# Moving two groups of activation tiles off the 64-byte grid of SBUF

## The chip, the cores and the metric

The kernel runs on one core of a Trainium2 chip. Its five engines are TensorE (PE in the profile; its weight loads are listed apart as PEld), VectorE (DVE), ScalarE (ACT), GpSimd (POOL) and SyncE (SP), and they work side by side, held in order by semaphores. The metric is the device time of one execution in microseconds; the median of several runs is given.

## The reference

Inputs are in float32, and the weights arrive as 64-bit values that the kernel decodes itself. Three stages follow one another over 8 batches of 576 rows with 512 features:

```python
# linear attention, 8 heads of 64
q_s = softmax(q, axis=-1); k_s = softmax(k, axis=2)
x = einsum('bhsd,bhde->bhse', q_s, einsum('bhsd,bhse->bhde', k_s, v))    # then heads side by side
# gated convolution
gate = sigmoid(causal_conv(x, conv_w))        # 5 taps along the sequence
y = (gate * (x @ w_val)) @ w_out
# channel mix; y_prev is y one row earlier
xk = mu_k * y + (1 - mu_k) * y_prev
xr = mu_r * y + (1 - mu_r) * y_prev
out = sigmoid(xr @ w_r) * (relu(xk @ w_k) ** 2 @ w_v)     # w_k: 512 x 1024, w_v: 1024 x 512
```

## The kernel before

The 4,608 rows are cut into 12 chunks of T = 384. Features lie on the 128 partitions, the rows of a chunk along the free axis, so a tile of activations is 128 x 384 and a chunk has 4 of them for 512 features.

The first chunk (i == 0) runs in float32 with one matmul for each product. For the other 11 chunks every operand a is split into a high part h (rounded to the type float32r, by ScalarE) and a low part l = a - h (by VectorE), and a product becomes three matmuls: h by h, h by l, l by h. `passes` (line 449) issues all of them, so almost every matmul of the kernel stands under line 449 and is told apart by its tiles. In the profile `ph<-xkh,wk_hi` is output, moving operand, stationary operand. Each matmul is preceded by a load of its own 128 x 128 stationary block.

The products of a chunk, in this order:

- **px** is the attention's output: moving operand q, stationary the attention's k-v matrix. It is copied to xf (5 taps need 4 earlier rows, so its data begins 4 words into the tile) and split into the pair xh, xl.
- **pv** is x by w_val: moving operand xh or xl, 384 columns. VectorE multiplies it with the gate into gf, which is split into gh, gl.
- **py** is the gated value by w_out: moving operand gh or gl, 384 columns. ScalarE copies it to yf (one earlier row ahead of the data). `mix` makes xm from it twice: for w_r, split into xrh, xrl, and for w_k, split into xkh, xkl.
- **racc** is xr by w_r: here the weights are the moving operand, 512 columns, and 128-column slices of xrh or xrl are stationary.
- **ph** is xk by w_k in 8 blocks: moving operand xkh or xkl, 384 columns. Relu and square give rf, split into kh, kl.
- **vacc** is the square by w_v: weights moving, 512 columns, slices of kh or kl stationary.

The main products of a chunk are issued in this order on TensorE; the attention of the next chunk, the convolution and the key-value rounds are put between them by two lists written by hand (`FRONT` for the start, `REST` for chunks 2 to 11).

Tiles are taken from pools by tag; each tag has a number of buffers of fixed place that are used in turn. Tag "x" (8 buffers in the pool `work`) holds xh, xl, and later in the same chunk xrh, xrl. Tag "g" (8 buffers, alone in the pool `gated`) holds gh, gl, and later xkh, xkl. In the first chunk single tiles of the same tags hold the whole values. Tags "q" and "k" are in `work` too. `pair_of` makes pairs, `one` single tiles. Pools on the left lie behind each other in SBUF in the order in which they are opened, and four tiles that nobody reads serve as gaps: left_gap, before_gap (ahead of the g tiles), behind_gap (behind them) and right_gap.

Of the kernel before, what the change touches and what calls it, by code (L numbers as in the profile page):

```python
# [8 lines left out]
F32 = mybir.dt.float32  # L9
F32R = mybir.dt.float32r  # L10
# [56 lines left out]
def tile_linear_attention_gated_conv_channel_mix(  # L67
# [21 lines left out]
    P = 128  # L89
    NC = DM // P  # L90
    NF = DFF // P
    T = 384
# [15 lines left out]
    work = ctx.enter_context(tc.tile_pool(name="work", bufs=1))  # L108
    gatep = ctx.enter_context(tc.tile_pool(name="gated", bufs=1))


    wts.tile([P, LEFT_GAP // 4], F32, name="left_gap")
    gatep.tile([P, 16], F32, name="before_gap")
    ends = ctx.enter_context(tc.tile_pool(name="ends", bufs=1, side="right"))
    ends.tile([P, RIGHT_GAP // 4], F32, name="right_gap")
    behind = ctx.enter_context(tc.tile_pool(name="behind", bufs=1))
    behind.tile([P, 48], F32, name="behind_gap")


    first_ctx = ctx.enter_context(ExitStack())  # L120
# [187 lines left out]
    def kv_max(st):  # L308
        kt = st["k"]
        pm = scratch("pm")[:, 0:HR * D]  # L310
        one = pm.rearrange("p (h d) -> p h d", d=D)
        nc.vector.tensor_max(one, kt[:, :, 0, :], kt[:, :, 1, :])
        for x in range(2, NST):
            nc.vector.tensor_max(one, one, kt[:, :, x, :])
        st["pm"] = pm
# [105 lines left out]
    def q_norm(st, h=slice(0, H)):  # L421
# [6 lines left out]
        nc.vector.reciprocal(qs, qs)  # L428
        nc.vector.tensor_mul(qt, qt, q4.rearrange("p t (h o) -> p t h o", o=1).to_broadcast([P, NT, n, D]))

    def pair_of(tag, bufs, pool=work):
        return lambda name: tuple(pool.tile([P, T], F32R, tag=tag, bufs=bufs, name=name + x) for x in "hl")

    x_pair, g_pair, q_pair, k_pair = pair_of("x", 8), pair_of("g", 8, gatep), pair_of("q", 2), pair_of("k", 8)

    def one(tag, bufs, name):
        return (gatep if tag == "g" else work).tile([P, T], F32, tag=tag, bufs=bufs, name=name)

    def split(a, pair):

# [40 lines left out]
    def x_take(st, i, c):  # L481
        pq = st["pq", c]
        if i < 2:
            qf, = st["q", c] = (one("q", 2, "q"),)
            if i:
                nc.scalar.copy(qf, pq[:, :T])
            else:
                nc.scalar.copy(
                    qf.rearrange("c (p t) -> c p t", t=NT), pq[:, :T].rearrange("c (t p) -> c p t", t=NT)
                )  # L490
            return
        qh, ql = st["q", c] = q_pair("q")
        nc.scalar.copy(qh, pq[:, :T])  # L493
        nc.vector.tensor_sub(ql, pq[:, :T], f32(qh))  # L494
# [313 lines left out]
```

## Time and profile before

| what | us |
|---|---|
| median of 3 runs | 812.14 |
| lowest and highest run | 810.77, 812.4 |
| span of the profiled execution, first to last instruction | 810.1 |
| TensorE busy in it | 798.3 |
| weight loads (overlap with TensorE's matmuls) | 701.2 |
| VectorE busy | 564.5 |
| ScalarE busy | 479.3 |
| GpSimd busy | 59.2 |

The profiled execution has no other time of its own than its span. Matmuls are pipelined: one starts before the recorded end of the one ahead of it, so the pace is read from start to start, or from a run of matmuls and its length, and not from the duration of one. Durations of one are given in ns, all else in us.

### The profile page before, as it was taken

What the parts mean: (1) busy time and instruction counts of PE and PEld (TensorE: products, weight loads), DVE (VectorE), ACT (ScalarE), POOL (GpSimd) and SP (SyncE); (2) the same over time, 40 slices, a digit from 0 to 9 for tenths busy, and PEclk for the clock granted to TensorE, in tenths of its full rate; (3) what the DMA queues carried; (4) which work ended last, traced back from release to release, by engine and by line L of the source; (5) the groups of instructions that cost most, each with busy time, mean ns of one, the idle gap of its engine ahead of it and who ended that gap; (6) DMA issues with size and microseconds to landing.
All of it is one profiled execution on the core that took longest, in us unless ns stands there. A gap on an engine that the chain in (4) does not pass through costs nothing.

```text
span 810.1 us, 12242 instructions
## 1 busy us (share of the span) xinstructions
PE 798.3 (99%) x4578; PEld 701.2 (87%) x4578; DVE 564.5 (70%) x1016; ACT 479.3 (59%) x948; POOL 59.2 (7%) x224
## 2 busy tenths in 40 slices
PE   6999999999999999999999999999999999999998
PEld 5545588999999999989989999999999999998996
DVE  7999889976777577577758577577576747644611
ACT  4667678637746746655754763763764674664542
POOL 2130001000002001000000100100000100100000
PEclk9999999999999999999999999999999999999999
DMA  9786220132222102013041211211222010000001
GB/s 310 244 269 217 59 78 1 40 98 59 75 63 59 40 27 72 7 36 91 7 98 46 53 40 39 60 39 40 59 65 73 1 37 23 22 1 14 26 1 40
DMA packets 92537, 53.25 MB, mean 66 GB/s; under 512 B 74018, under 2 KB 84286, under 8 KB 92478
## 3 DMA queue, kind: packets, MB, share of 16 engines
q1 hardware_dynamic: 92432, 52.44, 22.3%
q8 instruction: 36, 0.59, 0.3%
q14 instruction: 23, 0.19, 0.1%
q10 hardware_dynamic: 46, 0.02, 0.0%
HBM read 43.02 MB, written 9.44 MB: 65 GB/s over the span
## 4 chain that ended last, share of the span: by engine, by line
PE 95%; DMA 2%; DVE 1%; ACT 1%; SPq 1%; issue 0%; ACTq 0%
PE ph L449 25%; PE vacc L449 25%; PE racc L449 12%; PE pv L449 12%; PE py L449 12%; PE px L449 4%; PE kvacc L347 2%; PE pq L476 2%; DMA raw<-in_moe_w_val_dram 1%; DMA raw<-in_moe_w_k_dram 1%; DVE gate L548 1%; DMA kt<-in_k_dram 1%; PE mx L333 0%; PE pmT L321 0%; SPq L303 0%; DVE whole L152 0%
## 5 line engine op out<-in xcount | busy, mean ns | idle before, releaser
L548 DVE SCALAR_TENSOR_TENSOR gate<-xf,cw,gate 128x384 f32<-128x384 f32 x192 | 117.2, 615 | 5.1 <-ACT gate L546 2.3
L449 PE MATMUL ph<-xkh,wk_hi 128*128 128x384 f32 x352 | 120.3, 342 | 0.0
L449 PE MATMUL ph<-xkl,wk_hi 128*128 128x384 f32 x352 | 118.3, 336 | 0.0
L449 PE MATMUL ph<-xkh,lower 128*128 128x384 f32 x352 | 118.1, 336 | 0.0
L642 ACT ACTIVATE rf<-ph 128x384 f32<-128x384 f32 x96 | 46.8, 488 | 99.0 <-PE ph L449 98.1
L449 PE MATMUL vacc<-wv_hi,kh 128*128 128x512 f32 x264 | 104.0, 394 | 0.0
L449 PE MATMUL vacc<-lower,kh 128*128 128x512 f32 x264 | 103.2, 391 | 0.0
L449 PE MATMUL vacc<-wv_hi,kl 128*128 128x512 f32 x264 | 103.1, 391 | 0.0
L442 DVE TENSOR_TENSOR kl<-rf,kh 128x384 fp32r<-128x384 f32 x88 | 48.9, 556 | 70.1 <-ACT kh L441 69.1
L616 DVE SCALAR_TENSOR_TENSOR xm<-yf,mus,xm 128x384 f32<-128x384 f32 x96 | 56.5, 614 | 24.2 <-ACT xm L615 23.7
L449 PEld LDWEIGHTS ph<-xkh,wk_hi 128*128 128x128 f32 x352 | 66.2, 188 | 2.0 <-ACT xkh L441 0.2
L449 PEld LDWEIGHTS ph<-xkh,lower 128*128 128x128 f32 x352 | 66.2, 188 | 1.9
L449 PEld LDWEIGHTS ph<-xkl,wk_hi 128*128 128x128 f32 x352 | 66.1, 188 | 0.0
L494 DVE TENSOR_TENSOR ql<-pq,qh 128x384 fp32r<-128x384 f32 x40 | 22.2, 556 | 62.5 <-ACT qh L493 62.5
L441 ACT CAST gh<-gf 128x384 fp32r<-128x384 f32 x44 | 22.5, 511 | 72.0 <-DVE gf L589 72.0
L449 PE MATMUL py<-gh,wout_hi 128*128 128x384 f32 x176 | 59.6, 343 | 0.0
L449 PE MATMUL pv<-xh,lower 128*128 128x384 f32 x176 | 59.5, 338 | 0.0
L449 PE MATMUL pv<-xh,wval_hi 128*128 128x384 f32 x176 | 59.5, 338 | 0.0
L449 PE MATMUL pv<-xl,wval_hi 128*128 128x384 f32 x176 | 59.3, 337 | 0.0
L449 PEld LDWEIGHTS vacc<-wv_hi,kl 128*128 128x128 f32 x264 | 49.5, 188 | 11.0 <-DVE kl L442 0.3
L449 PE MATMUL py<-gl,wout_hi 128*128 128x384 f32 x176 | 58.2, 339 | 0.0
L449 PE MATMUL py<-gh,lower 128*128 128x384 f32 x176 | 58.0, 338 | 0.0
(132 smaller groups left out, 1723.0 us busy)
## 6 DMA issues: line engine op xcount, KB each, us to landing
out_dram<-rs SPq DMA_DIRECT2D x36, 256.0 KB, 2.0
kt<-in_k_dram SPq DMA_DIRECT2D x16, 512.0 KB, 4.5
qt<-in_q_dram SPq DMA_DIRECT2D x29, 256.0 KB, 3.4
vt<-in_v_dram SPq DMA_DIRECT2D x56, 128.0 KB, 3.6
raw<-in_moe_w_k_dram SPq DMA_DIRECT2D x8, 512.0 KB, 5.5
raw<-in_moe_w_v_dram SPq DMA_DIRECT2D x8, 512.0 KB, 6.8
raw<-in_moe_w_val_dram SPq DMA_DIRECT2D x4, 512.0 KB, 6.3
raw<-in_moe_w_out_dram SPq DMA_DIRECT2D x4, 512.0 KB, 8.4
```

The source lines that it names most:

```text
L347: nc.tensor.matmul(acc[e * D:(e + 1) * D, x * VW:(x + 1) * VW], lhsT=kt[:, 2 * x + e, s, :], rhs=st["v"][:, 2 * x + e, s, :], start=(s == ...
L441: nc.scalar.copy(pair[0], a)
L442: nc.vector.tensor_sub(pair[1], a, f32(pair[0]))
L449: nc.tensor.matmul(po, lhsT=left[a], rhs=right[b], start=start and x == 0, stop=stop and x == len(m) - 1)
L476: nc.tensor.transpose(pq[:, t * P:(t + 1) * P], qt[:, t, 2 * c:2 * c + 2, :].rearrange("p h d -> p (h d)"), f32(ident))
L494: nc.vector.tensor_sub(ql, pq[:, :T], f32(qh))
L548: nc.vector.scalar_tensor_tensor(out=gx(gate), in0=xv[:, :, HALO - sh:HALO - sh + L], scalar=tap(c, HALO - sh), in1=gx(gate), op0=ALU.mult ...
L616: nc.vector.scalar_tensor_tensor(out=gx(xf), in0=yv[:, :, 1:], scalar=mu[:, c:c + 1], in1=gx(xf), op0=ALU.mult, op1=ALU.add)
L642: nc.scalar.activation(rf, ph[:, :T], AF.Relu)
```

## The change

Tiles of tag "x" are made 16 words longer than their 384 words of data, and the data begins 4 words (16 bytes) into the tile. The gap ahead of the g tiles grows from 16 to 24 words and the gap behind them shrinks from 48 to 40, so the g tiles move by 32 bytes against what lies ahead of and behind their pool. The instructions, their order, the number of buffers and all waits stay as they are.

```diff
-    gatep.tile([P, 16], F32, name="before_gap")
+    gatep.tile([P, 24], F32, name="before_gap")
     ends = ctx.enter_context(tc.tile_pool(name="ends", bufs=1, side="right"))
     ends.tile([P, RIGHT_GAP // 4], F32, name="right_gap")
     behind = ctx.enter_context(tc.tile_pool(name="behind", bufs=1))
-    behind.tile([P, 48], F32, name="behind_gap")
+    behind.tile([P, 40], F32, name="behind_gap")
...
+    SHIFT = {"x": 4}
+
+    def shifted(pool, dtype, tag, bufs, name):
+
+        o = SHIFT.get(tag, 0)
+        return pool.tile([P, T + 4 * o], dtype, tag=tag, bufs=bufs, name=name)[:, o:o + T]
+
     def pair_of(tag, bufs, pool=work):
-        return lambda name: tuple(pool.tile([P, T], F32R, tag=tag, bufs=bufs, name=name + x) for x in "hl")
+        return lambda name: tuple(shifted(pool, F32R, tag, bufs, name + x) for x in "hl")
...
     def one(tag, bufs, name):
-        return (gatep if tag == "g" else work).tile([P, T], F32, tag=tag, bufs=bufs, name=name)
+        return shifted(gatep if tag == "g" else work, F32, tag, bufs, name)
```

## Rows read from the trace of the kernel before

**Rows 1.** Page, parts 1 and 4: busy time of TensorE; the chain's shares.

```profile
PE 798.3 (99%) x4578; PEld 701.2 (87%) x4578; DVE 564.5 (70%) x1016; ACT 479.3 (59%) x948; POOL 59.2 (7%) x224
...
PE 95%; DMA 2%; DVE 1%; ACT 1%; SPq 1%; issue 0%; ACTq 0%
PE ph L449 25%; PE vacc L449 25%; PE racc L449 12%; PE pv L449 12%; PE py L449 12%; PE px L449 4%; PE kvacc L347 2%; PE pq L476 2%; DMA raw<-in_moe_w_val_dram 1%; DMA raw<-in_moe_w_k_dram 1%; DVE gate L548 1%; DMA kt<-in_k_dram 1%; PE mx L333 0%; PE pmT L321 0%; SPq L303 0%; DVE whole L152 0%
```

**Rows 2.** Busy time by stretch; the first line names the columns.

```profile
core 0: us, PE busy (x) PEld busy (x) DVE busy (x) ACT busy (x) POOL busy (x), PEclk, DMA share, GB/s
...
160.00:800.00 640.00, 640.00 (x3797) 589.08 (x3796) 418.53 (x751) 369.75 (x740) 37.48 (x154) 1.00 0.16 43
```

**Rows 3.** Waits of weight loads: who for whom, us in total, times, longest.

```profile
PEld vacc L449 <- issue: 7.2, 30, 0.2
PEld racc L449 <- issue: 3.8, 16, 0.2
```

**Rows 4.** Chain that ended last, in order of time: start us, us, what.

```profile
60.11 6.13 PE ph L449 x19
...
686.50 8.32 PE pv L449 x48
694.82 8.47 PE py L449 x48
703.29 8.17 PE racc L449 x36
...
772.95 6.24 PE ph L449 x36
```

**Rows 5.** Timeline, 773.49 to 773.83 us: start us, us, engine, instruction.

```profile
773.49 0.33 PE L449 MATMUL ph<-xkh,lower 128*128 128x384 f32 x1
773.49 0.19 PEld L449 LDWEIGHTS ph<-xkl,wk_hi 128*128 128x128 f32 x1
773.65 0.34 PE L449 MATMUL ph<-xkl,wk_hi 128*128 128x384 f32 x1
773.66 0.19 PEld L449 LDWEIGHTS ph<-xkh,wk_hi 128*128 128x128 f32 x1
773.83 0.34 PE L449 MATMUL ph<-xkh,wk_hi 128*128 128x384 f32 x1
```

**Rows 6.** Views of tiles, elementwise work: ns min/median/max, first and last start us.

```profile
L514 ACT CAST xh<-xf x44: 501/515/536, 92.7 to 746.5; 128x384 fp32r<-128x384 f32 x44
L515 DVE TENSOR_TENSOR xl<-xf,xh x44: 550/552/569, 93.2 to 747.2; 128x384 fp32r<-128x384 f32 x44
...
L441 ACT CAST xkh<-xm x44: 496/510/518, 131.0 to 769.6; 128x384 fp32r<-128x384 f32 x44
L442 DVE TENSOR_TENSOR xkl<-xm,xkh x44: 547/556/559, 132.0 to 770.1; 128x384 fp32r<-128x384 f32 x44
...
L607 ACT ACTIVATE yf<-py x48: 469/492/495, 45.0 to 764.8; 128x384 f32<-128x384 f32 x48
...
L642 ACT ACTIVATE rf<-ph x96: 467/491/511, 64.3 to 799.9; 128x384 f32<-128x384 f32 x96
```

**Rows 7.** View of the tiles whole: float32 matmuls of the first chunk, columns as above.

```profile
L449 PE MATMUL ph<-xm,whole x64: 486/486/488, 58.4 to 97.6; 128*128 128x384 f32 x64
...
L449 PE MATMUL pv<-xf,whole x32: 486/486/590, 21.2 to 35.8; 128*128 128x384 f32 x32
...
L449 PE MATMUL py<-gf,whole x32: 486/486/590, 36.2 to 46.4; 128*128 128x384 f32 x32
```

**Rows 8.** Views of tiles: full-rate matmuls, one of three groups of each product.

```profile
L449 PE MATMUL pv<-xl,wval_hi x176: 334/334/422, 107.6 to 756.0; 128*128 128x384 f32 x176
...
L449 PE MATMUL py<-gh,wout_hi x176: 332/336/445, 115.6 to 764.1; 128*128 128x384 f32 x176
...
L449 PE MATMUL racc<-wr_hi,xrh x132: 389/389/397, 124.5 to 772.1; 128*128 128x512 f32 x132
...
L449 PE MATMUL ph<-xkh,wk_hi x352: 332/336/445, 133.1 to 799.2; 128*128 128x384 f32 x176
```

## The prediction

> **What bounds the kernel now.** I read the page first. TensorE is busy for 798.3 of 810.1 us, and the chain that ended last is PE for 95% of the span, almost all of it line 449, the helper that issues the products [rows 1]. The table of stretches then shows that this is no average over different limits: from 160 to 800 us PE is busy for all of 640.0 us, VectorE for 418.5, ScalarE for 369.8, and the clock granted to PE is 1.00 of full speed, its 2.4 GHz level [rows 2]. Of the waits of weight loads the longest in total, 7.2 us in 30 pieces, is one for nothing but the issue [rows 3]. So for this change the time is a count of matmuls times the pace of one, and what VectorE or ScalarE do faster or slower costs nothing until PE has to wait for it.
>
> The pace of one matmul is read from the chain in order of time, where a run of matmuls stands with its length. 36 of ph take 6.24 us, so 173.3 ns from one start to the next, 48 of pv take 8.32 us, also 173.3, and 36 of racc take 8.17 us, 226.9 [rows 4]. At 2.4 GHz 384 columns would pass in 160.0 ns and 512 in 213.3. Each matmul thus costs 13.3 to 13.6 ns, 32 clocks, more than its columns, and that excess is the same for both widths. The 20 single-pass products of the first chunk (float32, which runs at half the column rate, so 320.0 ns for 384 columns) do not show it: 19 take 6.13 us, 322.6 each, an excess of 2.6 ns [rows 4]. The timeline shows what goes on during the excess: each weight load starts within 0.01 us of the matmul before its own and takes 0.19 us, so one is always reading SBUF while PE streams the moving operand at full rate [rows 5]. My reading, an inference, is that the two streams of PE get in each other's way: 32 clocks for each load, and nearly nothing when the moving stream runs at half the rate.
>
> **The change part by part.** Adding up the tiles in the order of the code, every operand of a full-rate matmul now starts on a multiple of 64 bytes: x tiles at 132,608 + 1,536 n, g tiles at 157,248 + 1,536 n, weights on multiples of 256. Afterwards x starts 16 bytes past the grid (a tile is 64 bytes longer, so the step between tiles is 1,600 bytes), g 32 bytes past it (the gap ahead grows by 32, the one behind shrinks by 32). All that lies behind x moves by 512 bytes, so k, kvf and the upper weights stay on the grid. No instruction, transfer, wait or buffer is added or removed.
>
> Elementwise work on shifted tiles: nothing. The same subtraction takes a median of 552 ns (xl, whose source xf starts 16 or 48 bytes past the grid) and 556 ns (xkl, both sources on it) [rows 6]. ScalarE's cast takes 515 ns from the off-grid xf and 510 from xm, on the grid [rows 6]. As a destination: yf, written at 4 bytes past a multiple of 32, takes 492 ns from PSUM, rf, on the grid, 491 [rows 6]. Both signs stay within 5 ns; it hides under PE, of whose window these engines fill 65% and 58% [rows 2]. Without that cover 5 ns on the casts and subtractions that write x or g (eight groups of 44, four of them in [rows 6]) would be 1.8 us; I take 0.
>
> Products of the first chunk that read x or g in float32: nothing. pv there reads xf 16 or 48 bytes off the grid and takes a median of 486 ns, py and ph on the grid 486 as well [rows 7]. At half rate the start makes no difference.
>
> Full-rate products with x or g as moving operand are the change. pv is 3 x 176 = 528 matmuls on x; py is 528 and ph 3 x 352 = 1,056 on g, so 1,584 [rows 8]. No row has such a matmul off the grid, so its price is bounded. At best the excess falls to that of the half-rate rows: 13.3 - 2.6 = 10.7 ns on 2,112 matmuls, -22.6 us. At worst a row of 1,536 bytes that touches 25 groups of 64 bytes instead of 24 pays for the extra group: 16 columns, 6.7 ns, +14.1 us. Between the two I take the shift itself: the moving stream meets the load's reads 16 bytes, 4 columns, 1.67 ns elsewhere for x, and 8 columns, 3.33 ns for g. That size has a neighbour in the trace: one and the same ph matmul takes 332 ns at least and 336 in the median, though every operand is on the grid [rows 8], and one step in the timeline reads 0.16 us, where 173.3 ns must read 0.17 or 0.18 [rows 5]. So where in each other the two streams start is worth some 4 ns. For the sign I take a gain, which is an assumption: with both streams on the grid, each load runs the longest it can in step with the moving stream. Terms: 528 x 1.67 = 0.9 us, 1,584 x 3.33 = 5.3 us.
>
> racc: 396 matmuls with x as stationary operand and weights as moving [rows 8]. There the load moves and the stream stays: 1.67 ns either way, 0.7 us. I take 0.
>
> The sum is -6.2 us. Against the profiled execution's span of 810.1 us that gives 803.9; its time is not listed apart from the span, and the median of the three runs, 812.14, stands 2.0 us above it, so the forecast is 812.1 - 6.2 = 806.0 us. Nothing is late instead: in py, the products that wait for VectorE's gf and its split, 48 matmuls take 8.47 us, 0.15 us over pv's [rows 4], and that wait starts at pv's end whatever pv's pace is.
>
> [...]
>
> **The rivals.** *No change: the streams settle into one pace whatever the start.* For it: pv's x tiles lie on multiples of 128 bytes, ph's g tiles 64 past one, and both take 173.3 ns [rows 4]; the short step in the timeline is made up for in the next one, 0.18 us [rows 5]. Against it: all those starts are equal modulo 64, which is what changes now. Time: 812.1 us. [...]
>
> *Slower: the 25th group.* If PE fetches 64 bytes at a time, an off-grid row needs one fetch more for each matmul, 16 clocks: 2,112 x 6.67 ns = 14.1 us, 826.2 us; half hidden, 819. It decides from 0.77 ns per matmul (1.6 us over 2,112). For it: at full rate there is no slack, the stream is what sets the pace. Against it: the half-rate pv with an off-grid xf shows none of it, 486 against 486 ns [rows 7].
>
> *The edit does not shift what counts*, because the excess is not the meeting of two reads but a fixed price of changing weights at this data type; then the time is that of the first rival, 812.1. Against it: half-rate products change weights as often and pay 2.6 ns [rows 4].
>
> **How the numbers follow.** The gain has a chance of 0.49 (its own range is 797 to 810: a few tenths of a us up to two and a half times the sum), no change 0.29 with both reasons for it, the extra fetch 0.22. A measurement of this kernel can tell about 0.2%, 1.6 us, from no change, so these are also the chances of faster, same and slower. The likeliest is 806.0. The range runs from 797 to 819: it leaves out the part of the gain that nears the half-rate bound, some 0.07, and the extra fetch where none of it hides, some 0.11.
>
> **What would show it.** In the chain in order of time, ph and py would fall from 173.3 to about 170 ns per matmul and pv to 171.7, with racc at 226.9 and vacc unchanged. The medians of ph's and py's rows would fall by 3 to 4 ns, those of xkl, gl and the casts by nothing. ph at 180 would be the extra fetch; ph at 173.3 with steps still settling would be the first rival. The prediction is wrong if the streams' relative start decides nothing, or if x and g answer with opposite signs: then -0.9 and +5.3 or the reverse would have to be read apart. A new wait of weight loads for VectorE or ScalarE of more than a microsecond would say that elementwise work, which I cost at nothing, has come onto the path.

## The result: 1% slower, with the sign of the forecast turned

The changed kernel takes 820.12 us (median of 4 runs, 819.36 to 820.55) against 812.25 for the kernel before; the ratio is 1.0099, 95% interval 1.0085 to 1.0113. The forecast was 806.0 us, with a range of 797 to 819 and a chance of 0.22 for slower. The profiled execution has a time of 819.36 and a span of 817.4 us, 7.3 more than before. Of the experiments below one run, the profiled one of e10, took 1,621.34 us, about twice its other four; it is left out of e10's ratio, and e10's chain is read from a further run of the same kernel, e12.

The page of the changed kernel, parts 1 and 4, against [rows 1]:

```profile
PE 806.5 (99%) x4578; PEld 706.8 (86%) x4578; DVE 564.7 (69%) x1016; ACT 479.6 (59%) x948; POOL 58.2 (7%) x224
...
PE 98%; ACT 0%; DVE 0%; issue 0%
PE ph L456 25%; PE vacc L456 25%; PE py L456 13%; PE pv L456 13%; PE racc L456 13%; PE px L456 3%; PE kvacc L347 3%; PE pq L483 2%; PE heat L745 1%; PE pmT L321 0%; PE mx L333 0%; ACT q L495 0%; DVE rs L666 0%; DVE pm L314 0%; DVE raw L151 0%
```

The same 4,578 matmuls keep PE busy 8.2 us longer; VectorE and ScalarE work as long as before, to 0.3 us. Line 449 is line 456 now. Waits of weight loads are where they were, against [rows 3]:

```profile
PEld vacc L456 <- issue: 7.2, 30, 0.2
PEld racc L456 <- issue: 3.8, 16, 0.2
```

So it is the pace. The chain in order of time, last chunk (start us, us, what), against [rows 4]:

```profile
754.35 8.42 PE pv L456 x48
762.77 8.59 PE py L456 x48
771.36 8.38 PE racc L456 x36
779.74 6.36 PE ph L456 x36
786.09 2.08 PE vacc L456 x9
...
807.09 6.44 PE vacc L456 x27
```

ph went from 173.3 to 176.7 ns (6.36 us / 36), pv to 175.4, py by 2.5 ns, and racc, in which no moving operand was shifted, from 226.9 to 232.8 ns. vacc, whose operands are on the grid before and after, takes 2.08 us for the 9 matmuls behind the 36 of ph where before, in the same place of the chunk, the chain has

```profile
779.19 2.05 PE vacc L449 x9
...
799.86 6.44 PE vacc L449 x27
```

and 6.44 us for 27 in both: vacc loses a little at its beginning and nothing later. The groups by line and form (count | busy us, mean ns of one) give the amounts; here the three groups of ph, after and then before:

```profile
L456 PE MATMUL ph<-xkh,wk_hi 128*128 128x384 f32 x352 | 121.4, 345 | 0.0
L456 PE MATMUL ph<-xkl,wk_hi 128*128 128x384 f32 x352 | 119.2, 339 | 0.0
L456 PE MATMUL ph<-xkh,lower 128*128 128x384 f32 x352 | 118.9, 339 | 0.0
```

```profile
L449 PE MATMUL ph<-xkh,wk_hi 128*128 128x384 f32 x352 | 120.3, 342 | 0.0
L449 PE MATMUL ph<-xkl,wk_hi 128*128 128x384 f32 x352 | 118.3, 336 | 0.0
L449 PE MATMUL ph<-xkh,lower 128*128 128x384 f32 x352 | 118.1, 336 | 0.0
```

Summed over the three groups of each product, after less before: ph 359.5 - 356.7 = 2.8 us and, from the same view, pv 1.3, py 1.0, racc 2.1, vacc 1.2. Together that is 8.4 us; PE's whole busy time grew by 8.2, as px fell by 0.2. Elementwise work on shifted tiles costs nothing, as forecast, against [rows 6] (min/median/max ns):

```profile
L448 ACT CAST xkh<-xm x44: 495/508/517, 129.9 to 776.0; 128x384 fp32r<-128x384 f32 x44
L449 DVE TENSOR_TENSOR xkl<-xm,xkh x44: 543/556/561, 130.9 to 776.6; 128x384 fp32r<-128x384 f32 x44
```

And the float32 matmuls of the first chunk, against [rows 7], keep 486 ns with g 32 bytes off the grid. (The 16 products of py in that chunk are listed as 32 matmuls, so each float32 product runs as two; what the prediction calls single-pass products are these halves.)

```profile
L456 PE MATMUL py<-gf,whole x32: 486/486/590, 35.7 to 45.9; 128*128 128x384 f32 x32
```

The excess in the prediction rests on a column rate of 2.4 a ns, in float32 half of it. The profile gives the clock as a share of full speed, 1.00 in [rows 2], and not in GHz; the rates are read from products of different widths. In float32 the chain of before has 162.5 ns for 192 columns (px), 322.5 for 384 (ph) and 429.0 for 512 (vacc), so 1.20 columns a ns from each to the next:

```profile
75.81 2.58 PE ph L449 x8
...
90.94 0.65 PE px L449 x4
...
103.12 4.29 PE vacc L449 x10
```

At full rate a matmul of racc takes 53.6 ns more than one of ph (226.9 against 173.3, [rows 4]) for 128 columns more: 2.39 columns a ns, if both widths have the same excess. At these rates 384 columns take 160.8 ns and 320.0 in float32, and the excess is 12.5 and 2.5 ns (estimates from these paces), where the prediction has 160.0, 320.0, 13.3 and 2.6. Its "32 clocks" are the 13.3 ns at 2.4 a ns and no reading of their own.

### The profile page after: what moved, and what is told of

It reads as the page before. It is cut to its first block, busy times and chain, and to the rows that moved or that the text cites. A ratio compares the mean times of both kernels' runs of the same rounds, so it can differ in the third digit from the quotient of the medians.

```text
span 817.4 us, 12242 instructions
## 1 busy us (share of the span) xinstructions
PE 806.5 (99%) x4578; PEld 706.8 (86%) x4578; DVE 564.7 (69%) x1016; ACT 479.6 (59%) x948; POOL 58.2 (7%) x224
## 4 chain that ended last, share of the span: by engine, by line
PE 98%; ACT 0%; DVE 0%; issue 0%
PE ph L456 25%; PE vacc L456 25%; PE py L456 13%; PE pv L456 13%; PE racc L456 13%; PE px L456 3%; PE kvacc L347 3%; PE pq L483 2%; PE heat L745 1%; PE pmT L321 0%; PE mx L333 0%; ACT q L495 0%; DVE rs L666 0%; DVE pm L314 0%; DVE raw L151 0%
```

## Experiments

Every kernel is the one before with the lines shown (the two called "off" further down are the changed one), and its ratio is against the kernel before on the same chip. "Place" is a tile's start modulo 128 bytes. Before, x and all weights stand at place 0 and g at 64; after the change xh stands at 16, xl at 80, g at 96. `PAD` is the number of words by which a tile is longer than its 384.

**Each part alone.** `e1_g_alone` has the change's gaps and leaves x as it was.

```diff
-    gatep.tile([P, 16], F32, name="before_gap")
+    gatep.tile([P, 24], F32, name="before_gap")
-    behind.tile([P, 48], F32, name="behind_gap")
+    behind.tile([P, 40], F32, name="behind_gap")
```

> Only the g tiles lie 32 bytes off the grid; x is on it. Relative theory (a matmul's pace depends on where its moving operand and the stationary block that loads beside it stand to one another within 64 bytes): ph goes from 173.3 to 176.7 ns (12 in 2.12 us) and py with it, pv and racc stay at 173.3 and 226.9, vacc behind ph loses some 1 us in all; about +5.5 us, 817.7. Far-address theory (what costs is that k, kvf and the upper weights moved by 512 bytes): ph and vacc stay as before, 812.

Ratio 1.0072 (1.0057 to 1.0087), 818.0 us. Its chain, last chunk:

```profile
753.62 8.34 PE pv L449 x48
761.97 8.58 PE py L449 x48
770.55 8.20 PE racc L449 x36
778.75 6.36 PE ph L449 x36
785.11 2.08 PE vacc L449 x9
```

py, ph and vacc are slow, pv is as before and racc but for 0.03 us. `e2_x_alone` shifts x alone:

```diff
+    SHIFT = {'x': 4}
+    PAD = {'x': 16}
...
+        o = SHIFT.get(tag, 0)
+        return pool.tile([P, T + PAD.get(tag, 0)], dtype, tag=tag, bufs=bufs, name=name)[:, o:o + T]
...
```

> Only the x tiles lie 16 bytes off the grid. Relative theory: pv goes from 173.3 to about 175.4 ns (48 in 8.42 us), racc, where x is the stationary operand, from 226.9 to 232.8 (36 in 8.38 us), ph, py and vacc stay; about +3 us, 815. Far-address theory: vacc and ph slow down too, since k and the upper weights move by 512 bytes here as in the change; about +8 us, 820.

Ratio 1.0038 (1.0023 to 1.0053), 815.58 us:

```profile
751.01 8.42 PE pv L457 x48
...
767.90 8.39 PE racc L457 x36
776.29 6.25 PE ph L457 x36
782.54 2.05 PE vacc L457 x9
```

Here pv and racc are slow and the rest is as before, though k and the upper weights have moved by the 512 bytes of the change. The far-address theory is gone, and the parts add up: the groups by form gain 5.2 us in e1 and 3.4 in e2, 8.6 against the change's 8.4, and the ratios gain 0.72% and 0.38%, 1.10% against 0.99%, which is within their intervals.

**Moved, but on the grid.** `e3_moved_on_grid` is e2 with `SHIFT = {'x': 0}`: x tiles 1,600 bytes apart as in the change, all on multiples of 64, xh at place 0 and xl at 64.

> x tiles are 64 bytes longer, but their data begins at the start of the tile: every tile moves as in the change, and all stay on the 64-byte grid. Relative theory: no change, 812, ph 12 in 2.08 us, vacc 9 in 2.05. Far-address theory: vacc 9 in 2.08 us as after the change, some 1 to 8 us slower.

Ratio 1.0025 (1.0015 to 1.0034), 813.59 us. Neither theory had it: ph and vacc are as before, but the products on x are not.

```profile
748.72 8.38 PE pv L457 x48
...
765.57 8.33 PE racc L457 x36
773.90 6.24 PE ph L457 x36
```

So standing on the 64-byte grid is not enough to keep the pace. The longer step, which puts high and low part 64 bytes apart modulo 128, slows racc to 231.4 ns by itself. The change did this to x by the way, through the longer tile.

**Everything off the grid.** `e4_all_by_32` and `e5_all_by_32_even` move every operand of the three-matmul products, weights too, 32 bytes off the 64-byte grid. In e4 the pools on the right go the other way, so wval, wout and wr's high parts stand at place 96 and their low parts at 32; in e5 all move by the same 32 bytes, so that every distance is as before.

```diff
-LEFT_GAP, RIGHT_GAP = 32, 224
+LEFT_GAP, RIGHT_GAP = 64, 256        # e4; in e5: 64, 192
```

> Every operand of a full-rate matmul, weights too, lies 32 bytes off the grid; none is off relative to another. Relative theory: no change, 812, ph 12 in 2.08 us. Absolute theory (an off-grid operand costs by itself, as by a 25th group of 64 bytes): ph, py, pv, racc, vacc and px all slow down, by 3 to 6 ns each, 3,500 matmuls: +10 to +20 us, 822 to 832.

> Every operand of a full-rate matmul lies 32 bytes past a multiple of 64 and, unlike in e4_all_by_32, every one keeps its distance to every other modulo 128 (all at 32, g at 96). Relative theory, with distances counted modulo 128 from one matmul to the next as well: the pace of before everywhere, pv, py, ph 173.3 ns, racc 226.7, 812. Absolute theory (off the 64-byte grid costs by itself): pv, py and racc as slow as in e4, 175.4, 175.7 and 233.9 ns, about 818.

e4: ratio 1.0070 (1.0055 to 1.0085). ph and vacc, whose weights have both parts at 32, are as before; pv, py and racc, whose weights have not, are the slow ones, although every distance there is 0 or 64 modulo 128. e5: ratio 1.0017 (1.0006 to 1.0027), and its chain, last chunk, is that of before to 0.01 us:

```profile
748.28 8.34 PE pv L449 x48
756.62 8.47 PE py L449 x48
765.09 8.17 PE racc L449 x36
773.26 6.24 PE ph L449 x36
779.51 2.05 PE vacc L449 x9
```

An off-grid start by itself costs no run of matmuls there anything. That removes the extra fetch for a 25th group of 64 bytes, the prediction's slower rival: in e5 every moving row of 1,536 bytes touches 25. The 0.17% of e5's runs stand in no line of its profile (span 810.5 us) and stay unexplained.

**Other distances.** With `PAD` 32 the tiles of a tag are a multiple of 128 bytes apart, so that high and low part have one place (modulo 256 they now stand 128 apart, where before they were equal).

```diff
+    SHIFT = {'x': 4, 'g': 4}         # e6; in e7: 12 and 12
+    PAD = {'x': 32, 'g': 32}
...
-    gatep.tile([P, 16], F32, name="before_gap")      # e8: both gaps out, SHIFT = {'x': 8}, PAD = {'x': 32}
+    gatep.tile([P, 8], F32, name="before_gap")       # e9: 8 and 56, x as before
```

> x and g both 16 bytes past the grid against weights on it, with tiles 128 bytes longer, so that high and low part lie equal modulo 128. Relative theory: ph and py leave 173.3 ns for about 176, racc 226.7 for 230 or more, pv 173.3 for about 176; about +7 us, 819. By the alternating part alone (high and low part 64 bytes apart modulo 128, as in the change) pv and racc would be back at 173.3 and 226.7, and only ph and py slow. By the size of the shift, as the prediction had it, ph would lose half of what 32 bytes cost, 1.7 ns.

> x and g both 48 bytes past the grid, high and low part equal modulo 128. Relative theory: the same as 16 bytes, or with the sign turned for racc, where x is stationary: all four products slower than before, about 819. If some distance other than a multiple of 64 gives a faster pace than 173.3 ns, it is this one or the 16 bytes of e6_both_by_16: then ph at 170 ns, 12 in 2.04 us, and about 805.

> x 32 bytes past the grid, high and low part equal modulo 128; g on a multiple of 128 as the weights are, instead of 64 past one. Relative theory: ph and py stay at 173.3 ns (a distance of 0 settles as one of 64 does), pv goes to 176 to 177 and racc to 230 to 233; about +3.5 us, 815.5. If a distance of 64 was itself worth something, ph and py change with it.

> Only g is off the 64-byte grid, by 32 bytes as in e1_g_alone, but 32 past a multiple of 128 where the change has it 96 past one; x and weights on multiples of 128. If the distance of moving operand to stationary block counts modulo 64, this is e1_g_alone again: ph 176.7 ns, about 817.7. If it counts modulo 128 and with its sign (pv with x at 32 kept 173.6 ns in e8_x_by_32_g_on_128), ph and py settle at 173.3 ns, 36 in 6.24 us, and the time is 812 to 814, what is left being the matmuls before the pace has settled.

Ratios: e6 1.0085 (1.0070 to 1.0100), e7 1.0086 (1.0069 to 1.0103), e8 1.0074 (1.0059 to 1.0089), e9 1.0041 (1.0026 to 1.0056). Two last versions put k at place 64, e10 and e11, and x too in e10 (`SHIFT` 16, `PAD` 32); if distances modulo 128 were all, they would have beaten the kernel before.

> All activations lie 64 bytes past a multiple of 128, where g lies before, and the weights on one. Distances modulo 128: every product settles at 173.3 or 226.7 ns; vacc, whose first matmuls behind ph take 229 to 233 ns before, starts settled: 9 in 2.04 us instead of 2.05, about -1 us, 811. If a stationary operand at 64 bothers the load, racc and vacc are slower than before, 230 ns or more, and the time is 814 or more.

> Only k, the stationary operand of vacc, is moved to 64 past a multiple of 128; x as before. Distances modulo 128: pv, racc, py, ph as before, vacc as in e10_k_and_x_at_64, about -1 us, 811. What e10 shows more or less than this belongs to x.

> The kernel of e10_k_and_x_at_64 once more, for its profile. If 64 bytes are free for a moving operand that stands ahead of its stationary block and not the other way round, as g in ph before (free) and k in vacc in e11_k_at_64 (2.08 us for 9) say: pv 48 in 8.34 us as before, racc 36 in 8.3 us or more, vacc 9 in 2.08. If only k is bothered, racc stays at 8.17.

e10 1.0049 (1.0036 to 1.0063), e11 1.0019 (1.0008 to 1.0030), e12 816.19 us in one run beside 812.28. None is faster than before. Each kernel's chain in its last chunk, us for the run of matmuls (e10's from e12):

| kernel | places (x; g; k) | pv x48 | py x48 | racc x36 | ph x36 | first vacc x9 |
|---|---|---|---|---|---|---|
| before | 0; 64; 0 | 8.34 | 8.47 | 8.17 | 6.24 | 2.05 |
| change | 16 and 80; 96; 0 | 8.42 | 8.59 | 8.38 | 6.36 | 2.08 |
| e1 | 0; 96; 0 | 8.34 | 8.58 | 8.20 | 6.36 | 2.08 |
| e2 | 16 and 80; 64; 0 | 8.42 | 8.47 | 8.39 | 6.25 | 2.05 |
| e3 | 0 and 64; 64; 0 | 8.38 | 8.47 | 8.33 | 6.24 | 2.05 |
| e4 | all + 32; right weights + 96 | 8.43 | 8.55 | 8.42 | 6.24 | 2.05 |
| e5 | all + 32 | 8.34 | 8.47 | 8.17 | 6.24 | 2.05 |
| e6 | 16; 80; 0 | 8.43 | 8.55 | 8.38 | 6.32 | 2.08 |
| e7 | 48; 112; 0 | 8.46 | 8.52 | 8.30 | 6.30 | 2.08 |
| e8 | 32; 0; 0 | 8.33 | 8.49 | 8.39 | 6.26 | 2.08 |
| e9 | 0; 32; 0 | 8.34 | 8.47 | 8.18 | 6.36 | 2.04 |
| e10 | 64; 64; 64 | 8.39 | 8.47 | 8.34 | 6.24 | 2.08 |
| e11 | 0; 64; 64 | 8.35 | 8.48 | 8.17 | 6.24 | 2.08 |

No run of matmuls in the table is shorter than before by more than 0.01 us, so no pace is below the 173.3 and 226.9 ns of before as far as the chain can tell. Distances of 16, 48, 80, 96 and 112 slow their products (in the change, e2, e6, e7 and, for g, e1: pv to 8.42 to 8.46 us, py to 8.52 to 8.59, racc to 8.30 to 8.39, ph to 6.30 to 6.36); 32 and 64 bytes are free for some and not for others. x 32 bytes ahead of the weights leaves pv at 8.33 us and slows racc, in which x is the stationary operand, to 8.39 (e8); g 32 ahead leaves py's 8.47 and slows ph, on tiles of the same tag, to 6.36 (e9). 64 is free in ph and py (6.24 and 8.47), costs pv little (8.39 in e10), and is not free in racc (8.34 in e10) or vacc (2.08 in e11), where the stationary operand is the one that stands ahead. But in e6 to e8, e10 and e11 the tiles that were shifted were made longer as well, by 128 bytes, and no run has that step without a shift; after e3 the step is a rival explanation for racc and vacc there, untested. In e8, ph settles but its beginnings cost: 36 in a row take 6.26 us and 12 take 2.10 where before they take 2.08, and the vacc behind short runs of ph takes 2.08 for 2.05. And one distance can have two paces: in e9, 12 ph take 2.12 us behind racc, in all nine such places, and 2.08 or 2.09 behind the transposes pq, in all 19, with g's tiles and the weights at the same places:

```profile
450.58 8.20 PE racc L449 x36
458.78 2.12 PE ph L449 x12
460.90 0.65 PE pq L476 x6
461.56 2.08 PE ph L449 x12
```

It is not the blocks of ph that differ: in the last chunk, without transposes between them, 36 in a row take 6.36 us, three times 2.12. In the kernel before both are 2.08, in e1 both 2.12 (one 2.11). No one rule for the distance comes out of this, and distance alone does not fix the pace.

**Which stream is it?** Four kernels take one of PE's two streams out of its walk through SBUF. ph's moving operand is one column read 384 times, or its stationary block one column read 128 times, in the layout of before ("grid") and in the changed one ("off"). In these, ph's values, and what follows from them, are not the reference's.

```diff
-            product(ph[:, :T], "wk", f * P, [st["xk", c] for c in range(NC)])
+            product(ph[:, :T], "wk", f * P, [tuple(a[:, 0:1].to_broadcast([P, T]) for a in st["xk", c]) if i else st["xk", c] for c in range(NC)])
...
+                w = tuple(a[:, 0:1].to_broadcast([P, P]) for a in w) if i else w
```

> Layout of before. In the 11 chunks of three matmuls ph's moving operand is one column of xkh or xkl read 384 times, so ph's values are not the reference's. Meeting-streams theory: the moving stream stays in one place and the pace of ph leaves 173.3 ns, towards 162.6 (the half-rate rows' excess of 2.6 ns) if it meets the load rarely, or above 173.3 if it stands where every load passes. Fixed-price theory (32 clocks for changing weights at this data type): 173.3 ns, 36 in 6.24 us.

> The same with the changed layout: ph's moving operand one column read 384 times. If a walking moving stream is needed for the start of a tile to matter, ph has here the pace of still_moving_grid and not 3.3 ns more. If only the start of the instruction counts, it is 3.3 ns slower than there.

> Layout of before. In the same chunks ph's stationary block is one column of W_k's part read 128 times, so ph's values are not the reference's. Meeting-streams theory: the load reads one place, meets the moving stream less, and ph's pace falls below 173.3 ns, at best to 162.6: up to -11 us. Fixed-price theory: 173.3 ns, 812.

> The same with the changed layout. Meeting-streams theory: ph has the pace of still_stationary_grid, for with a load that does not walk there is no distance left to count. Fixed-price theory: the change's 176.7 ns.

With a still moving operand, one run each: 801.92 and 806.67 us, the kernel before beside them 811.35. The chain of still_moving_off, in the changed layout:

```profile
751.51 8.59 PE py L456 x48
760.10 8.38 PE racc L456 x36
768.48 5.88 PE ph L456 x36
...
778.40 2.05 PE vacc L456 x9
```

ph takes 163.3 ns (5.88 us / 36), in still_moving_grid the same:

```profile
763.66 5.88 PE ph L449 x36
```

The layout no longer matters to it, it is 10.0 ns faster than before, which leaves 3.3 of the 13.3 ns over the prediction's 160.0, and py and racc beside it still have the change's slow pace. vacc behind the short runs of ph is back at 2.05 without any change to itself, and its three groups by form at 310.6 us, where the change has 311.5 and the kernel before 310.3: what it loses in the change it inherits from ph.

With a still stationary block, 813.79 and 817.64 us. The chain of still_stationary_off:

```profile
770.09 8.38 PE racc L456 x36
778.47 6.24 PE ph L456 x36
784.71 2.04 PE vacc L456 x9
```

ph has 173.3 ns in the changed layout, and the same 6.24 us in still_stationary_grid. There vacc shows the inheritance the other way round: in the layout of before, behind this ph, it is slow.

```profile
774.47 6.24 PE ph L449 x36
780.71 2.08 PE vacc L449 x9
784.87 2.09 PE vacc L449 x9
```

The layout no longer matters here either, but the pace stays at 173.3 ns and with it the excess of 13.3. The expectation of a gain of up to 11 us from a still load was wrong.

So 10.0 of the 13.3 ns are there only with a moving operand that walks through SBUF (173.3 against 163.3 ns), and also with a load that does not (173.3). The 3.3 ns of the layout (176.7 against 173.3) are there only when both walk. That is shown for ph, in one run of each kernel. Whether the excess needs the load at all is open: each of the 4,578 matmuls has one, and no run was without.

## Why the prediction was wrong

*The bound and the count held.* The time is the number of matmuls times their pace, no other engine came onto the path, and 2,112 moving and 396 stationary uses of x and g were the ones to look at.

*The step that failed is the sign*: "For the sign I take a gain, which is an assumption: with both streams on the grid, each load runs the longest it can in step with the moving stream." The runs show the opposite: of all layouts tried none has a pace below that of before, 173.3 ns for 384 columns and 226.9 for 512, as far as the chain can tell, and in the changed kernel no product that reads x or g keeps it (pv 175.4, py 2.5 ns more, ph 176.7, racc 232.8). That the streams run "in step" in one layout and not in the other is a reading; no run shows it. The forecast size for g's 32 bytes, 3.33 ns, is what ph lost (6.36 against 6.24 us for 36), but its working, columns of the shift, is not borne out: 16 bytes in e6 cost ph 2.2 ns and 48 in e7 cost 1.7, not half and three halves.

*The reading behind it*, called an inference, was that the 13.3 ns over the columns are the load and the moving stream getting in each other's way. No run shows that meeting itself. The 3.3 ns of the layout agree with it, as they go when either stands still; the 13.3 ns do not as it was put: with a still stationary block ph keeps 173.3 ns, with a still moving operand it has 163.3. Why a walking moving operand costs 10 ns stays open.

*The row that should have warned of it* was in the prediction: one step of 0.16 us was made up for by the next one. Steps that come back to one pace speak for a settled one; that a shift is likelier to disturb it than to better it is my estimate, and no layout tried here bettered the 173.3 ns. I read the rows as room on both sides.

*racc, taken as 0, cost 2.1 us*, the second largest term. 1.67 ns "either way" was the bound; 5.8 ns were measured. Part of that is no offset but the longer tile: e3, with the longer tile alone, has racc at 8.33 of the change's 8.38 us. That high and low part of one value came to stand 64 bytes apart modulo 128 stood in the prediction only as "the step between tiles is 1,600 bytes", without a price.

*vacc, taken as unchanged, cost 1.2 us*, by inheritance, which the prediction's terms had no place for: it priced each product by its own operands. With a still ph in the changed layout vacc is back within 0.3 us of the kernel before (310.6 against 310.3).

*The rivals.* "No change" is refuted by ph alone, which left 173.3 ns for 176.7. The extra fetch had the right sign and the wrong mechanism: 14.1 us by its own working, 7.9 measured, and e5 removes it. That the edit does not shift what counts because the excess is a price for changing weights: still_moving_grid, which loads as many weights, has 163.3 ns.

*The range* ended at 819, 1.1 us short, because its upper end came from half the extra fetch, with racc at 0 and vacc left out. Those two are 3.3 us.

## What to carry to other kernels

Where TensorE sets the time with full-rate matmuls of 4-byte operands, treat the starts of moving and stationary tiles as one system: look at runs of matmuls in the chain, and if they settle at one pace, as here at 173.3 and 226.9 ns, keep all distances, and those between the tiles of one stream, as they are: in e5 all operands of the products moved together by 32 bytes and every product kept its pace to 0.01 us in its run of matmuls. That only the distances modulo 128 have to be kept was not shown. A pad of 64 bytes per tile changes them, even when every tile stays on the 64-byte grid (e3, 0.25% slower). And price a product by what runs ahead of it too: here the first 9 matmuls of vacc took 2.05 us behind the ph of before and 2.08 behind that of the change, with vacc's tiles at the same places.

## What the runs showed of the hardware that was not expected

- The pace of full-rate matmuls falls to 163.3 ns for 384 columns when the moving operand is one column read again and again: 10 ns of each of ph's matmuls, and 9.4 us of the kernel in one run (811.35 to 801.92), are there only when the moving operand walks.
- Distances that are equal modulo 128 do not all cost the same: 64 bytes are free in ph and cost racc 0.17 us in 36 matmuls (e10) and vacc 0.03 in 9 (e11). Whether the sign, a larger modulus or the longer tiles of e10 and e11 make the difference was not tried.
- With g at place 32, ph has two paces in one kernel (e9): 176.7 ns behind racc and 173.3 or little more behind the transposes, with all places the same. So in e9 the pace differs with what ran ahead, for operands at unchanged places.
